# A new prologue order, a second issuer for a small load, and a split last copy in a fused attention and expert kernel on one core

## The chip, the cores and the metric

The kernel runs on one core of one Trainium2 chip. The core has five engines that matter here: TensorE (PE in the profile, with its weight loads as PEld), VectorE (DVE), ScalarE (ACT), GpSimd (POOL) and SyncE (SP). SP computes nothing in this kernel: it issues nearly all the transfers between the chip's main memory and the on-chip memory. Each engine takes its own instructions in the order in which the program lists them, and waits on semaphores for the others' results. The metric is the device time of one execution in microseconds; lower is better.

## The reference

There are 8 batches of 8 heads. Per head, `x` has 512 rows of 64 values and `state` 32 rows of 64. Rows of `x` attend to `state`, and rows of `state` attend to `x`; both results go, with the heads side by side, as 4352 rows of 512 values through a maxout layer:

```
scores = scale * x @ state.T              # 512 x 32 per head
a = softmax(scores);  xread = a @ state
scores2 = scale * state @ x.T             # the same products, transposed
a2 = softmax(scores2); sread = a2 @ x     # 32 x 64 per head
h = concat(xread, sread) over rows, heads side by side
out = maximum(h @ w1, h @ w2) @ w_out     # 512 -> 1024 -> 512
```

Inputs and output are float32.

## The kernel before

**The algebra.** The kernel never builds `h` for the `x` rows. Since `max(a, b) = relu(a - b) + b`, it forms `wd = w1 - w2` (tile `wd`, by `w_sub`) and `wwo = w2 @ w_out` (tile `wwo`, by `w_wo_mm` and `w_wo_ev`), so that `out = relu(h @ wd) @ w_out + h @ wwo`. And since `h = a @ state`, it multiplies the state of each batch into both matrices first (`sw_mm`, tile `sw`), after which a batch needs only its attention weights `a`, transposed (`aT`). Layer 1 is then `l1_mm` (line 426: two matmuls of 512 columns per 128 features) with a relu copy `l1_ev`; layer 2 is `l2_f` (line 442) plus `l2_open` (line 438) for the `wwo` part, both into one accumulator bank, copied out by `l2_out` and stored.

**The weights.** `w1`, `w2` and `w_out` come in four quarters (`load_w2(q)`, `load_w1(q)`, `load_wo(q)`, 512 KB each, lines 98 to 108). Quarter 0 comes in six half pieces of 256 KB (`load_h(j, w)`, lines 110 to 122; `w` is 2 for `w2`, 1 for `w1`, 0 for `w_out`). Each piece lands as float32 and is cast to bf16 by one of three engines: `w2_cast`, `wo_cast`, and for the halves `w2_cast_h`, `w1_cast_h`, `wo_cast_h`. The last letter of such a call is the engine: "A" ScalarE, "V" VectorE, "P" GpSimd. All these copies go through the helper `copy`, so that in the profile they stand under line 58 (ScalarE), 60 (VectorE) and 62 (GpSimd). For quarter 0 the difference is not needed: `sw_h_mm` (line 401) adds the products with `w1` and with the negated state and `w2`.

**The prologue** runs from the first instruction to `store(0)` and covers batch 0, the weights, and batch 1's attention. Its order is written out by hand, one call after another (lines 616 to 846); each call appends its instructions to the queues of its engines, so the list sets the order on every engine. Batch 0's `x` arrives in four pieces of two heads, and each goes through a cast (`cast_pair`), four transposes on PE (`xt_pair_mm`, line 200), a copy (`xt_pair_ev`), scores against the block-diagonal state (`scores_pair_mm`, line 218) and the exponential (`scores_pair_ev`). Weights go, quarter by quarter, through rounds: `w2_tr_mm(q)` transposes `w2`, `w_wo_mm(q, i)` (line 551) adds that quarter to `w2 @ w_out` for each of four row blocks `i` and needs the cast `wo(q)`; `sw_two_mm(q)` (line 387) needs `wd(q)`, the result of `w_sub(q)` (line 539), and makes the columns of `sw` for batches 0 and 1 together; two `l1_mm(0, f)` follow, and `l2_part(q, c)` (two matmuls of 512 columns, 573 to 576) adds the quarter to the four output accumulators `c` of batch 0. For quarter 0, `w_wo_h_mm(i, j)` (line 556) and `w2_tr_h_mm` (line 519) work by halves.

`idle(n)` (line 571) issues `n` matmuls of 256 columns on zeros. Their results are not used.

**The banks.** PE's results go to eight banks of accumulator memory, four in the pool `ps` and four in `pa`. A new result in a pool waits until an older one has been copied out. The four accumulators of `l2_part` take the `pa` banks.

**State.** Batches 0 and 1 have their own small loads (`load_state(0)`, `load_state(1)`, 64 KB each, line 127, issued by ScalarE), a cast (`copy(.., sb0[:, b], sf0[:, b])`), a transpose (`state_mm`, line 132) and two copies into the block-diagonal tile `sbd` (`state_ev`). `state0_neg` makes the negated copy for batch 0 (line 143). Batches 2 to 7 come together (`load_states`, `states_cast`, `states_mm`, `states_ev`).

**The transfers.** SP issues the loads in the order in which they are listed (579 to 606). A transfer's completion is signalled on one of eight semaphores taken in turn, so that each issue waits for the transfer eight places before it; some also wait until the buffer that they fill has been read. `load_w2(3)` fills the buffer that `w_sub(0)` reads last.

**The loop** over batches 1 to 7 (line 849) is the same for each: scores of the next batch, its softmax (`norm_sums`, `norm_mul`), its transposes by transfer, four layer 2 accumulators (`l2`), the next batch's `sw`, then its layer 1. In the last batch the rows of `sread` go through the layers as well (`moe_sread`), and the last accumulator is done in two halves of 256 columns, each copied out and stored by itself (`l2_last`, 456 to 469).

Of the kernel before, what the change touches and what calls it, by code (L numbers as in the profile page):

```python
# [15 lines left out]
def kernel(  # L16
# [107 lines left out]
    P = {}  # L124

    def load_state(b):
        nc.scalar.dma_start(out=sf0[:, b].rearrange("p (j d) -> p j d", j=2),
                            in_=state[b].rearrange("(k j) n d -> n k j d", j=2))
# [327 lines left out]
    def l2_last(b, c):  # L456

        dst = out[b * L:b * L + S].rearrange("(p c) n -> p c n", c=NC)
        for h in range(2):
# [8 lines left out]
            copy("AV"[h], OB[b][:, c, cs], p[:, 0:256])  # L468
# [111 lines left out]
    load_state(1)  # L580
# [3 lines left out]
    load_x(0, 4, 3)  # L584
    load_h(0, 2)
    load_h(0, 1)
    load_h(0, 0)
    load_h(1, 1)
    load_h(1, 2)
# [5 lines left out]
    load_w1(2)  # L595
    load_w2(3)
    load_wo(2)
# [18 lines left out]
    idle(15)  # L616
    cast_pair(0, 0, "V")
    copy("A", sb0[:, 0], sf0[:, 0])
    xt_pair_mm(0, 0, pa)
    cast_pair(0, 1, "V")  # L620
    idle(3)
    state_mm(0, None)
    xt_pair_ev(0, 0, "V")
    xt_pair_mm(0, 1, pa)
    copy("A", sb0[:, 1], sf0[:, 1])
    state_mm(1, pa)
    cast_pair(0, 2, "P")
    xt_pair_ev(0, 1, "V")
    state_ev(0, "A")
    idle(3)  # L630
    scores_pair_mm(0, 0, pa)
    cast_pair(0, 3, "V")
    xt_pair_mm(0, 2)
    xt_pair_ev(0, 2, "V")
    state_ev(1, "A")
    state0_neg("P")
    scores_pair_ev(0, 0)
    reduce_pair(0, 0)
    scores_pair_mm(0, 1, pa)
    scores_pair_ev(0, 1)  # L640
    reduce_pair(0, 1)
    w2_cast_h(0, "P")
    idle(1)
    xt_pair_mm(0, 3)
    norm_sums(0, 0, False)
    norm_mul(0, 0, "P")
    xt_pair_ev(0, 3, "A")
    idle(1)
    scores_pair_mm(0, 2, None)
    wo_cast_h(0, "P")  # L650
    scores_pair_ev(0, 2)
    reduce_pair(0, 2)
    idle(5)
    scores_pair_mm(0, 3, pa)
    scores_pair_ev(0, 3)
    w2_tr_h_mm(0)
    w1_cast_h(1, "P")
    w1_cast_h(0, "A")
    idle(3)
    sread_mm(0, pa)  # L660
    idle(3)
    sw_h_mm(0, pa)
    reduce_pair(0, 3)
    norm_sums(0, 1, False)
    norm_mul(0, 1, "V")
    w2_tr_h_ev(0, "A")
    sw_ev(0, 0, 128, 1, "A")
    idle(4)
    w_wo_h_mm(1, 0)
    at_mm(0, 0, pa)  # L670
    sw_ev(0, 0, 128, 0, "A")
    at_mm(0, 1)
    w_sub(0, 0, 4, "P")
    w_wo_h_mm(3, 0)
    w2_cast_h(1, "V")
    at_ev(0, 1, "V")
    sw_h_mm(1, pa)
    sw_ev(0, 128, 256, 1, "V")
    wo_cast_h(1, "V")
    w2_tr_h_mm(1)  # L680
    at_ev(0, 0, "A")
    l1_mm(0, 0)
    sw_ev(0, 128, 256, 0, "A")
    l1_mm(0, 1, pa)
    w_wo_h_mm(0, 0, pa)
    w2_tr_h_ev(1, "A")
    l1_ev(0, 1, "A")
    w_wo_h_mm(2, 0)
    l1_ev(0, 0, "V")
    w_wo_h_mm(3, 1)  # L690
    w_wo_ev(0, 3, "A")
    w2_cast(1, "P")
    w_wo_h_mm(0, 1)
    w_wo_h_mm(1, 1)
    w_wo_h_mm(2, 1)
    sread_norm(0)
    l2_part(0, 3)
    sw_mm(1, 0, FQ)
    w_wo_ev(0, 1, "A")
    sw_ev(1, 0, FQ, 1, "A")  # L700
    l2_part(0, 1)
    sw_ev(1, 0, FQ, 0, "A")
    l2_part(0, 0)
    w2_tr_mm(1)
    w_sub(1, 0, 4, "V")
    w2_tr_ev(1, "V")
    wo_cast(1, "P")
    sw_two_mm(1)
    sw_two_ev(1, 1, "V")
    w_wo_ev(0, 0, "A")  # L710
    l2_part(0, 2)
    w_wo_mm(1, 1)
    w_wo_ev(1, 1, "V")
    w_wo_ev(0, 2, "A")
    w_wo_mm(1, 2)
    sw_two_ev(1, 0, "A")
    l1_mm(0, 3)
    w2_cast(2, "P")
    l1_ev(0, 3, "A")
    l1_mm(0, 2)  # L720
    w_wo_mm(1, 3)
    w2_tr_mm(2)
    l1_ev(0, 2, "A")
    w_wo_ev(1, 2, "V")
    w_wo_mm(1, 0)
    l2_part(1, 1)
    w_sub(2, 0, 4, "V")
    l2_part(1, 0)
    w_wo_ev(1, 0, "V")
    w2_tr_ev(2, "A")  # L730
    sw_two_mm(2)
    sw_two_ev(2, 1, "A")
    sw_two_ev(2, 0, "A")
    l2_part(1, 2)
    w_wo_ev(1, 3, "V")
    w2_cast(3, "P")
    l2_part(1, 3)
    w_sub(3, 0, 4, "P")
    w2_tr_mm(3)
    l1_mm(0, 5)  # L740
    wo_cast(2, "V")
    w_wo_mm(2, 0)
    w_wo_ev(2, 0, "V")
    w2_tr_ev(3, "A")
    w_wo_mm(2, 2)
    l1_mm(0, 4)
    l1_ev(0, 5, "A")
    w_wo_mm(2, 3)
    w_wo_mm(2, 1)
    l1_ev(0, 4, "A")  # L750
    l2_part(2, 3)
    alloc_x(1, "P", big.tile([128, NC, 4, 132], BF16, tag="r", name="xo"))
    cast_pair(1, 1, "P")
    cast_pair(1, 0, "P")
    w_wo_ev(2, 2, "V")
    l2_part(2, 0)
    w_wo_ev(2, 3, "V")
    wo_cast(3, "A")
    sw_two_mm(3)
    sw_two_ev(3, 0, "A")  # L760
    w_wo_mm(3, 2)
    w_wo_ev(2, 1, "V")
    l2_part(2, 1)
    w_wo_mm(3, 0)
    sw_two_ev(3, 1, "V")
    cast_pair(1, 3, "P")
    l1_mm(0, 6)
    cast_pair(1, 2, "A")
    xt_mm(1, 0)
    w_wo_ev(3, 2, "V")  # L770
    w_wo_ev(3, 0, "V")
    xt_ev(1, 0, "V")
    l1_mm(0, 7)
    xt_mm(1, 1)
    l1_ev(0, 6, "A")
    l1_ev(0, 7, "A")
    xt_ev(1, 1, "A")
    w_wo_mm(3, 1)
    scores_mm(1, 0)
    w_wo_ev(3, 1, "V")  # L780
    w_wo_mm(3, 3)
    l2_part(3, 0)
    scores_mm(1, 1)
    l2_part(2, 2)
    states_cast("P")
    scores_ev(1, 0)
    cast_half(2, 0, "P")
    scores_ev(1, 1)
    w_wo_ev(3, 3, "V")
    sw_mm(0, FF, WC)  # L790
    sw_ev(0, FF, WC, 1, "A")
    sw_ev(0, FF, WC, 0, "A")
    norm_sums(1, 0)
    norm_mul(1, 0, "P")
    l2_part(3, 2)
    l2_part(3, 1)
    l2_part(3, 3)
    sw_mm(1, FF, WC)
    norm_sums(1, 1)
    sw_ev(1, FF, WC, 0, "A")  # L800
    sread_mm(1)
    norm_mul(1, 1, "P")
    l2_open(0, 3, ACC[3], False, True)
    l2_open(0, 2, ACC[2], False, True)
    l2_out(0, 3, ACC[3], "A")
# [110 lines left out]
```

## Time and profile before

| | us |
|---|---|
| median of 5 runs | 148.36 |
| the five runs | 147.72, 152.19, 148.66, 148.36, 147.77 |
| the profiled execution's own time | 147.72 |
| its span, first to last instruction | 145.9 |
| PE busy | 139.5 (96%) |
| DVE busy | 85.4 (58%) |
| ACT busy | 69.3 (47%) |
| POOL busy | 59.0 (40%) |
| first scores of batch 2 on PE (end of the prologue's part on PE) | 42.1 |
| end of PE's last matmul | about 142.6 |

All durations below come from the one profiled execution. Its page gives the busy time of each engine, the span cut into 40 slices of 3.65 us (each digit is the busy share of a slice in tenths), the chain of work that ended last, and groups of instructions by line. The trace behind it also lists each queue in order of time: start, duration, engine, line, operation, output tile and input tiles, shapes, and in brackets how long the engine sat idle before and what ended that. Matmuls are pipelined: one of 512 columns is listed with 0.38 us, but the next starts 0.216 us later, and some matmul records are missing. `idle` matmuls count as busy PE time.

### The profile page before, as it was taken

The numbers are of one execution on the slowest core, as the hardware profiler recorded it, in microseconds if no ns is written. First come the engines' busy times: TensorE is split into PE (matmuls) and PEld (weight loads), VectorE is DVE, ScalarE is ACT, GpSimd is POOL, SyncE is SP. The second block draws the span as 40 slices with busy tenths as digits, with TensorE's granted clock in tenths as the row PEclk, the third lists the DMA queues.
The fourth block names the chain that finished last, engine by engine and source line by source line (L and its number), as shares of the span: only waits on it lengthen the run. The fifth ranks groups of instructions, "written<-read, shape, count | busy, mean of one in ns | idle before, by whom it ended". The sixth has DMA issues, their size and how long they took to land.

```text
span 145.9 us, 3217 instructions
## 1 busy us (share of the span) xinstructions
PE 139.5 (96%) x1295; PEld 71.1 (49%) x1314; DVE 85.4 (58%) x172; ACT 69.3 (47%) x135; POOL 59.0 (40%) x80
## 2 busy tenths in 40 slices
PE   6998999999999999999999999999999999999990
PEld 4664454464554445444544544454445344754460
DVE  3499795877874648464854675376557464621111
ACT  4486857686971456326450825271537145511010
POOL 2289435767938433924291447226500500000000
PEclk9999999999999999999999999999999999999999
DMA  4999999994559988595948785787306032402423
GB/s 128 311 327 357 356 363 362 361 349 156 99 102 340 209 296 265 102 290 214 240 87 278 261 184 109 251 295 140 72 27 260 7 72 110 180 4 72 144 104 111
DMA packets 36639, 29.18 MB, mean 200 GB/s; under 512 B 20240, under 2 KB 33808, under 8 KB 35728
## 3 DMA queue, kind: packets, MB, share of 16 engines
q1 hardware_dynamic: 36080, 28.84, 66.7%
q8 instruction: 10, 0.16, 0.4%
q10 hardware_dynamic: 544, 0.13, 0.4%
q14 instruction: 5, 0.04, 0.1%
HBM read 15.34 MB, written 8.91 MB: 166 GB/s over the span
## 4 chain that ended last, share of the span: by engine, by line
PE 91%; DMA 3%; DVE 2%; issue 1%; ACTq 0%; ACT 0%
PE acc L442 37%; PE ps L426 17%; PE acc L438 8%; PE ps L551 4%; DMA sf<-in_state_dram 3%; PE ps L361 3%; PE ps L481 2%; PE acc L491 2%; PE ps L271 2%; PE acc L328 2%; PE acc L571 2%; PE acc L466 1%; DVE wo L60 1%; PE acc L426 1%; PE acc L489 1%
## 5 line engine op out<-in xcount | busy, mean ns | idle before, releaser
L442 PE MATMUL acc<-wo,r 128*128 128x512 bf16 x246 | 59.3, 379 | 0.4
L442 PEld LDWEIGHTS <-r 128*128 128x128 bf16 x248 | 23.8, 98 | 28.9 <-issue 0.6
L58 ACT COPY ob<-acc 128x512 f32<-128x512 f32 (+1 forms) x16 | 9.2, 572 | 48.1 <-PE acc L442 27.9
L426 PE MATMUL ps<-aT,sw 128*128 128x512 bf16 x117 | 27.7, 379 | 0.0
L294 POOL TENSOR_TENSOR a<-e,er 128x512 bf16<-128x512 bf16 x15 | 15.5, 1050 | 27.5 <-ACT e L276 20.8
L417 DVE TENSOR_SCALAR r<-ps 128x512 bf16<-128x512 f32 x26 | 18.0, 691 | 14.1 <-PE ps L426 14.0
L415 ACT ACTIVATE r<-ps 128x512 bf16<-128x512 f32 x33 | 19.7, 600 | 6.5 <-PE ps L426 5.8
L60 DVE COPY ob<-acc 128x512 f32<-128x512 f32 (+1 forms) x17 | 11.1, 652 | 16.0 <-PE acc L442 14.6
L426 PEld LDWEIGHTS <-sw 128*128 128x128 bf16 x128 | 12.1, 98 | 13.7
L62 POOL CAST xb<-xf 128x1024 bf16<-128x1024 f32 x12 | 12.4, 1040 | 15.3 <-DMA xf<-in_x_dram 15.3
L62 POOL CAST xo<-xf 128x512 bf16<-128x512 f32 x28 | 16.1, 615 | 6.0 <-DMA xf<-in_x_dram 5.6
L60 DVE CAST sw<-ps 128x512 bf16<-128x512 f32 x15 | 9.8, 687 | 12.0 <-PE ps L361 11.6
L438 PE MATMUL acc<-sw,aT 128*128 128x512 bf16 x49 | 15.5, 381 | 0.3
L58 ACT CAST sw<-ps 128x512 bf16<-128x512 f32 (+1 forms) x21 | 11.0, 573 | 2.5 <-PE ps L387 1.3
L287 DVE TENSOR_REDUCE es<-e 128x16 f32<-128x512 bf16 x14 | 9.2, 656 | 1.6 <-ACT e L276 1.6
L571 PE MATMUL acc<-wz 128*128 128x256 bf16 x38 | 7.5, 343 | 1.2 <-DVE ones L609 1.2
L276 ACT ACTIVATE e<-ps 128x512 bf16<-128x512 f32 x14 | 7.7, 597 | 0.8 <-PE ps L271 0.2
L438 PEld LDWEIGHTS <-aT 128*128 128x128 bf16 x62 | 5.0, 98 | 4.4
L551 PE MATMUL ps<-wo,w2t 128*128 128x512 bf16 x23 | 6.5, 380 | 0.2
L562 DVE TENSOR_TENSOR w2acc<-ps,w2acc 128x512 f32<-128x512 f32 x8 | 5.2, 687 | 1.6 <-PE ps L551 1.5
L539 POOL TENSOR_TENSOR wd<-w1f,w2f 128x1024 bf16<-128x1024 f32 x2 | 4.9, 2446 | 1.7 <-DMA w1f<-in_moe_w_dram 1.7
L571 PEld LDWEIGHTS <-wz 128*128 128x128 bf16 x38 | 4.1, 121 | 2.3 <-DVE ones L609 1.2
(111 smaller groups left out, 146.4 us busy)
## 6 DMA issues: line engine op xcount, KB each, us to landing
xf<-in_x_dram SPq DMA_DIRECT2D x14, 512.0 KB, 5.6
out_dram<-ob SPq DMA_DIRECT2D x7, 1024.0 KB, 4.2
w2f<-in_moe_w_dram SPq DMA_DIRECT2D x3, 512.0 KB, 7.6
w1f<-in_moe_w_dram SPq DMA_DIRECT2D x3, 512.0 KB, 9.4
wof<-in_moe_w_out_dram SPq DMA_DIRECT2D x3, 512.0 KB, 8.5
xf<-in_x_dram SPq DMA_DIRECT2D x4, 256.0 KB, 4.0
out_dram<-ob SPq DMA_DIRECT2D x3, 256.0 KB, 2.0
w2f<-in_moe_w_dram SPq DMA_DIRECT2D x2, 256.0 KB, 5.3
```

The lines of the kernel that those rows point to most:

```text
L58: nc.scalar.copy(o, i)
L60: nc.vector.tensor_copy(o, i)
L62: nc.gpsimd.tensor_copy(o, i)
L287: nc.vector.tensor_reduce(d["es"][:, hh], ev, axis=mybir.AxisListType.X, op=ALU.add)
L294: (nc.gpsimd if eng == "P" else nc.vector).tensor_mul(av, ev, d["er"][:, hh].unsqueeze(3).to_broadcast([128, 2 * NC, 2, Ns]))
L415: nc.scalar.activation(out=o, in_=p, func=ACTF.Relu)
L417: nc.vector.tensor_scalar(o, p, scalar1=0.0, scalar2=None, op0=ALU.max)
L426: nc.tensor.matmul(p, SW[b][:, g, f * 128:(f + 1) * 128], AT[b][:, g].rearrange("p c t -> p (c t)"), start=(g == 0), stop=(g == 1))
L438: nc.tensor.matmul(p, AT[b][:, g, c, :], SW[b][:, g, FF:WC], start=(start and g == 0), stop=(stop and g == 1))
L442: nc.tensor.matmul(p, R[b][:, f, c * 128:(c + 1) * 128], wo[:, f, :], start=(start and j == 0), stop=(stop and j == len(fs) - 1))
L551: nc.tensor.matmul(p, w2t[:, f, i, :], wo[:, f, :], start=(f == fs[0]), stop=(f == fs[-1]))
L571: nc.tensor.matmul(idle_p[0][:, 0:cols], wz[:, 0:128], wz[:, 0:cols], start=True, stop=True)
```

## The change

It has three parts.

1. `load_state(1)` is issued by SP instead of ScalarE, as the ninth of SP's loads. The half pieces of quarter 0 are loaded in another order (`w_out` first), and `load_wo(2)` goes ahead of `load_w2(3)`.
2. The whole list of the prologue is in another order, and some steps are on other engines. Moved to ScalarE: the casts of `w2` half 0 (from GpSimd), `w1` half 1 (from GpSimd) and `w_out` half 1 (from VectorE), and the negated state (from GpSimd). Moved to GpSimd: the casts of `w2` half 1 and of `w_out` quarter 2 (both from VectorE), and of state 1 (from ScalarE). Moved to VectorE: the cast of batch 0's third piece and one `norm_mul` of batch 1 (both from GpSimd). No weight cast is left on VectorE. There are 45 `idle` matmuls instead of 38. `sread_tr_mm(0)` goes from the end of the prologue to before `l1_mm(0, 0)`, and `l2_part(0, 2)` from round 0 to after `sw_two_ev(2, 0)`.
3. In `l2_last`, the last 256 columns are copied by ScalarE and VectorE, 128 columns each, instead of by VectorE alone.

```diff
-    def load_state(b):
-        nc.scalar.dma_start(out=sf0[:, b].rearrange("p (j d) -> p j d", j=2),
+    def load_state(b, q=nc.scalar):
+        q.dma_start(out=sf0[:, b].rearrange("p (j d) -> p j d", j=2),
...
-            copy("AV"[h], OB[b][:, c, cs], p[:, 0:256])
+            for e, c0, n in (("A", 0, 256),) if h == 0 else (("A", 0, 128), ("V", 128, 128)):
+                copy(e, OB[b][:, c, 256 * h + c0:256 * h + c0 + n], p[:, c0:c0 + n])
...
     load_state(0)
-    load_state(1)
     load_x(0, 4, 0)
...
+    load_h(0, 0)
     load_h(0, 2)
     load_h(0, 1)
-    load_h(0, 0)
+    load_h(1, 2)
+    load_state(1, nc.sync)
     load_h(1, 1)
-    load_h(1, 2)
     load_h(1, 0)
...
+    load_wo(2)
     load_w2(3)
-    load_wo(2)
```

The list after the change, from the first matmul to the end of round 1 on PE:

```
idle(15)
copy("A", sb0[:, 0], sf0[:, 0]); state_mm(0, None)
cast_pair(0, 0, "V"); state_ev(0, "A"); xt_pair_mm(0, 0, pa)
cast_pair(0, 1, "V"); idle(2); xt_pair_mm(0, 1)
state0_neg("A"); xt_pair_ev(0, 1, "A"); xt_pair_ev(0, 0, "V")
scores_pair_mm(0, 0, None); scores_pair_ev(0, 0)
cast_pair(0, 2, "V"); idle(2); xt_pair_mm(0, 2); xt_pair_ev(0, 2, "A")
scores_pair_mm(0, 1, pa); cast_pair(0, 3, "V"); idle(2); xt_pair_mm(0, 3, pa)
idle(3); scores_pair_mm(0, 2, pa); scores_pair_ev(0, 1); scores_pair_ev(0, 2)
reduce_pair(0, 0); xt_pair_ev(0, 3, "V"); idle(1)
scores_pair_mm(0, 3, pa); scores_pair_ev(0, 3)
w2_cast_h(0, "A"); idle(13); w2_tr_h_mm(0); sread_mm(0, pa); w1_cast_h(0, "A")
reduce_pair(0, 1); norm_sums(0, 0, False); w2_tr_h_ev(0, "A"); reduce_pair(0, 2)
idle(2); sw_h_mm(0, None); sw_ev(0, 0, 128, 0, "A"); sw_ev(0, 0, 128, 1, "A")
wo_cast_h(0, "P"); reduce_pair(0, 3); norm_sums(0, 1, False)
idle(4); w_wo_h_mm(2, 0, pa); norm_mul(0, 1, "V"); norm_mul(0, 0, "P")
w2_cast_h(1, "P"); w1_cast_h(1, "A"); at_mm(0, 0); at_mm(0, 1, pa)
copy("P", sb0[:, 1], sf0[:, 1]); state_mm(1, None); sread_norm(0)
w2_tr_h_mm(1, pa); w_wo_h_mm(1, 0, pa); w_sub(0, 0, 4, "P"); at_ev(0, 0, "V")
idle(1); sw_h_mm(1, None); w_wo_h_mm(3, 0); at_ev(0, 1, "A"); w2_tr_h_ev(1, "V")
w2_cast(1, "P"); sread_tr_mm(0, pa); wo_cast(1, "P"); l1_mm(0, 0, pa)
sw_ev(0, 128, 256, 1, "V"); sw_ev(0, 128, 256, 0, "A"); l1_mm(0, 1)
wo_cast_h(1, "A"); sread_tr_ev(0, "V"); l1_ev(0, 0, "A"); w_wo_h_mm(0, 0, pa)
state_ev(1, "V"); w_wo_h_mm(2, 1); w_wo_ev(0, 2, "A"); w_wo_h_mm(3, 1); w_wo_h_mm(0, 1)
sw_mm(1, 0, FQ); w_wo_h_mm(1, 1); sw_ev(1, 0, FQ, 0, "A"); w2_cast(2, "P")
l1_ev(0, 1, "V"); l2_part(0, 0); w_sub(1, 0, 4, "V"); w2_tr_mm(1)
sw_ev(1, 0, FQ, 1, "A"); l2_part(0, 3); w_wo_ev(0, 0, "A"); w2_tr_ev(1, "V")
sw_two_mm(1); l2_part(0, 1); w_wo_ev(0, 3, "A"); sw_two_ev(1, 1, "V")
w_wo_mm(1, 3); w_wo_ev(1, 3, "V"); sw_two_ev(1, 0, "A"); w_wo_mm(1, 1)
```

Before the change, the stretch that ends at the same place is this:

```
sw_h_mm(1, pa); sw_ev(0, 128, 256, 1, "V"); wo_cast_h(1, "V"); w2_tr_h_mm(1)
at_ev(0, 0, "A"); l1_mm(0, 0); sw_ev(0, 128, 256, 0, "A"); l1_mm(0, 1, pa)
...
w_wo_h_mm(3, 1); w_wo_ev(0, 3, "A"); w2_cast(1, "P")
w_wo_h_mm(0, 1); w_wo_h_mm(1, 1); w_wo_h_mm(2, 1); sread_norm(0)
l2_part(0, 3); sw_mm(1, 0, FQ); w_wo_ev(0, 1, "A"); sw_ev(1, 0, FQ, 1, "A")
l2_part(0, 1); sw_ev(1, 0, FQ, 0, "A"); l2_part(0, 0); w2_tr_mm(1)
w_sub(1, 0, 4, "V"); w2_tr_ev(1, "V"); wo_cast(1, "P"); sw_two_mm(1)
sw_two_ev(1, 1, "V"); w_wo_ev(0, 0, "A"); l2_part(0, 2); w_wo_mm(1, 1)
```

Further on, the rest of rounds 1 to 3 and batch 1's steps follow in both versions, in another order, with `l2_part(0, 2)` between `sw_two_ev(2, 0)` and `w_wo_mm(2, 3)`, `wo_cast(2, "P")` ahead of `w2_cast(3, "P")`, and `norm_mul(1, 1, "V")` after `norm_sums(1, 1)`.

## The prediction

> **What bounds the kernel now.** I read the page's slices first, then the chain that ended last, then the queues of the engines over the first 20 us.
>
> ```profile
> PE 139.5 (96%) x1295; PEld 71.1 (49%) x1314; DVE 85.4 (58%) x172; ACT 69.3 (47%) x135; POOL 59.0 (40%) x80
> PE   6998999999999999999999999999999999999990
> DMA  4999999994559988595948785787306032402423
> ```
>
> TensorE (PE) is full in every slice but the first, second and last, and a full slice may hold `idle` matmuls. The DMA engines are full for nine slices, about 33 us. The chain, asked over 10 to 20 us (start, duration, what), shows where the second slice's hole is:
>
> ```profile
> 12.42 0.29 DVE sw L60
> 12.71 1.73 DVE wo L60
> 14.45 0.04 issue
> 14.49 0.38 PE ps L556
> ...
> 17.63 0.70 DVE w2t L60
> 18.34 0.05 issue
> 18.38 1.04 PE ps L551 x4
> ```
>
> There are two stalls. At 14.49 PE waits 0.55 us for a VectorE weight cast. At 18.38 it starts round 1 of `w_wo_mm` (L551), and behind that start the chain names VectorE's `w2t` copy. But POOL's queue shows a second condition ending in the same moment:
>
> ```profile
> 11.63 2.53 POOL L539 TENSOR_TENSOR wd<-w1f,w2f 128x1024 bf16<-128x1024 f32 x1
> 14.11 1.23 POOL L62 CAST w2b<-w2f 128x1024 bf16<-128x1024 f32 x1
> 17.29 1.04 POOL L62 CAST wo<-wof 128x1024 bf16<-128x1024 f32 x1 [1.95 <-DMA wof<-in_moe_w_out_dram]
> 18.89 1.04 POOL L62 CAST w2b<-w2f 128x1024 bf16<-128x1024 f32 x1 [0.56 <-DMA w2f<-in_moe_w_dram]
> ```
>
> POOL sat 1.95 us until `wo(1)` landed at 17.29, and cast it until 18.33. L551 reads that tile, so it cannot start before about 18.38 however fast everything else is. The stretches confirm that the landing is set by bandwidth, not by issue (last columns: granted clock, DMA share, GB/s):
>
> ```profile
> 8.00:9.00 1.00, 1.00 (x19) 0.78 (x17) 0.85 (x3) 0.87 (x2) 0.61 (x1) 1.00 1.13 334
> 14.00:15.00 1.00, 0.51 (x3) 0.27 (x3) 1.00 (x3) 0.24 (x2) 1.00 (x2) 1.00 1.00 364
> 17.00:18.00 1.00, 1.00 (x26) 0.67 (x25) 0.49 (x2) 0.88 (x2) 0.71 (x1) 1.00 1.09 346
> ```
>
> After 18.38 PE is dense. I add up what it does until batch 2's first scores at 42.10: 84 matmuls of 512 columns at 0.216 (18.14), six groups of eight transposes at 0.45 (2.70), four groups of `sw` matmuls at 0.34 (1.36), scores, sread and two small transposes (0.93): 23.13 us of 23.72, the rest being about 0.1 after each group of narrow tiles. The loop from 42.10 to 142.5 repeats in 13.85 us without a hole. So time can come only from before 18.38, or from the tail.
>
> **The change part by part.**
>
> *Front, up to round 1.* PE's real work is the same in both orders, and up to round 1 it differs in one thing: ahead of its first `w_wo_mm(1,.)`, the old order has four `l2_part(0,.)`, the new one three; `l2_part(0,2)` now comes after `sw_two_ev(2,0)`. That is 2 x 0.216 = 0.43 us of PE work moved behind the 18.38 gate. In return `sread_tr_mm(0)`, one transpose (0.06), moves in front of it. If the gate stays, PE is 0.37 us behind from there on, and nothing after it has a hole to take that up.
>
> Does the gate stay? Ahead of `wo(1)` in the queue stand the same bytes: states 0 and 1 (0.13 MB), batch 0's x, the six half pieces and `w2(1)`, `w1(1)`; only their order differs, and the DMA engines are at 1.0 or above from 2 us on. I take 17.29 again. Bounds: POOL could be late by one 512 KB transfer's spacing (17.29 to 18.89, so 1.6 us at most); an earlier landing pays only until PE's own readiness, which is 17.98 (below), so it gains 0.40 at most.
>
> Is PE ready? My hand chain, with durations from the rows: x's third and fourth pieces land as now or a little sooner (6.3, 7.2); scores of pair 3 end at 8.9 (ACT's last `e` 9.4); ACT casts `w2` half 0 (0.61) to 10.0; 13 idles (0.107 each) hold PE to 10.25; transposes, sread, `sw_h_mm(0)` at 11.1; `w_wo_h_mm(2,0)` 11.8; `at_mm` 12.0; ACT casts `w1` half 1 after its two `sw` copies, 11.98 to 12.6; `sw_h_mm(1)` 13.1; `l1(0,0)`, `l1(0,1)` 13.65 to 14.5; ACT casts `wo` half 1 by 14.35, where VectorE now ends it at 14.44 (1.81 us, against 0.53 for its cast of `w2b` of the same size). This is where the exchanged casts meet: ScalarE takes three half-weight casts, `xt_ev` of pairs 1 and 2 and the negated state (0.4), and gives one state cast to POOL; VectorE loses two weight casts. So the removed slow cast is paid back nearly whole by a busier ScalarE: the new order's round 0 ends about where the old one does. `l2_part(0,3)` ends at 17.2; `wd(1)` is ready at 15.90 + 1.23 = 17.13 (VectorE, waiting on the same landing as now); `sw_two_mm(1)` 0.35, `l2_part(0,1)` 0.43: 17.98. It is 0.4 before the gate. The seven additional idles (38 to 45, 0.75 us) lie in waits for weights; with that cover gone they would cost 0.75 less the 0.4.
>
> At one place the trace speaks of a conflict. VectorE's 1.81 us cast ran wholly inside POOL's 2.53 us subtraction, and POOL's cast of `w1b` took 1.08 beside VectorE's `norm_mul`, against 0.61 alone. The Trainium skill, page "SBUF — State Buffer", says that the pair of ports which VectorE and GpSimd share is an exclusive lock, and that a VectorE instruction with two SBUF inputs contends with a GpSimd one that reads SBUF. By that rule the new order makes a new conflict: `norm_mul(1,1)` goes to VectorE (estimated 35.0) while POOL goes on to cast batch 2. A whole block of 1.04 by the rule would put it 0.2 past PE's arrival; by the 0.47 that the row shows it stays hidden.
>
> The sum goes without it: `at_mm(1,0)` needs `norm_mul(1,1)` at 36.8; 35.0 plus 0.96 is 35.96, cover 0.8. Loss bound, from VectorE's slowed cast (1.81 less 0.53, 1.28): 0.5.
>
> *State 1 on SP.* One issue of 0.68 leaves ACT's queue and ACT's table load (now from 2.15) starts that much sooner, but its next work is the state 0 cast, held by a landing at 3.94: worth nothing. SP's queue grows by 0.68 ahead of `w1` half 1 and the ten weight loads behind it. SP's issues now run more than 2 us ahead of the engines (`wo(1)` issued 8.51, landed 17.29), so 0.68 is covered; uncovered it costs 0.68. State 1 itself lands near 10.6 instead of 5.92. POOL casts it just before `w_sub(0)`, PE's `state_mm(1)` stands at 12.4 with `w2_tr_h_mm(1)` and the rest behind it: cover about 1 us.
>
> *Other moves.* `wo(2)` goes ahead of `w2(3)`, which waits 2.2 us on SP for POOL's `wd`; spacing of the landings (18.89, 21.89, 23.1) puts `wo(2)` at 21.9, POOL's cast at 22.9, PE's `w_wo_mm(2,3)` at about 23.5: cover 0.6. `w2(3)` at 23.1, cast by 24.2, read at 25.2. POOL's `w_sub(3)` ends at 27.0 in both; `sw_two_mm(3)` comes at 27.8. `states_cast`, batch 1's casts and the round 3 copies each keep 0.3 or more.
>
> *Tail.* The last 256 columns, 0.42 on VectorE (L60), become two 128-column copies side by side: VectorE 0.29 (its 128x128 `sw` row), ScalarE 0.27. Gain 0.13; bounds 0.15, and nothing if the store's wait for two engines takes it back.
>
> Sum: +0.43 - 0.06 - 0.13 = +0.24 us. The profiled execution took 147.72 (span 145.9), the fastest of the five, so 147.96 in its terms. The four runs without the 152.19 average 148.13, 0.41 above it, so I forecast 148.4 for a median.
>
> **The rivals.**
>
> *A late front (slower).* ScalarE takes over three half-weight casts (0.61 each) and works in order, so one late landing delays evictions behind it. If PE reaches `w_wo_mm(1,3)` after 18.9 instead of 17.98, more than the 0.4 of cover and 0.5 beyond, it decides. For it: ACT is 0.75 to 0.95 busy from 6 to 11 us already, and 13 idles in one block run whether needed or not. Against: the new order removes 1.28 of slowed cast. With 1.0 beyond the cover: 147.96 + 1.0, about 149.4 as a median.
>
> *A gate that opens early (faster).* `wo(1)` lands well before 17.29 because in truth the transfers are not served in order, and the front is 1 us ahead through the missing VectorE casts. Against: the DMA share above, and 14.35 against 14.44. Both would have to move to 17.3 for a gain of 0.8: 147.2, as a median 147.6.
>
> *No effect.* The moved `l2_part` falls into a hole that I don't see, or the gate varies by more than the term: 147.6 to 147.8, 148.1 as a median.
>
> **How the numbers follow.** Forecast 0.42, no effect 0.15, late front 0.31, early gate 0.12. A measurement here tells about 0.5% (0.74 us) from no change. The forecast and no effect end within it, save 0.03 at the slow edge; so same 0.54, slower 0.34, faster 0.12. The range: low lies just under the early gate's 147.6, at 147.5; high is the late front's 149.4 and some of the runs' spread (148.66 is 0.3 above the median), 149.6.
>
> **What would show it.** Right: POOL's `wo` cast still begins near 17.3 after a DMA wait, L551 (now L552) starts near 18.4 after PE has idled in all some 0.4 just before; batch 2's first scores near 42.5; the last VectorE copy near 0.29. Wrong: PE arrives at L552 with POOL's cast long done (late front), the cast starts before 16.5 (early gate), or a hole of 0.3 or more stands after 20 us, at `at_mm(1,0)` or `w_wo_mm(2,3)`.

## The result and the profile after

The changed kernel takes 148.69 us in the median (43 runs), the kernel before 148.28 us over 80 runs beside them. The ratio is 1.0028, with a 95% interval of 1.0017 to 1.0038: the change costs about 0.41 us (0.25 to 0.56). One run of the changed kernel took 820.28 us and seven of the 80 took 151 to 153; the ratios here leave such slow runs out, and those of the experiments are not the quotients of the two medians beside them. The profiled execution of the changed kernel took 149.00 us (span 147.2), a little above its median; that of before, 147.72, was near its fastest. So the two profiles differ by 1.28 us, three times what the change costs, and most of this section is about separating the two.

From the page after: the busy time of each engine, then PE's busy share and the DMA share in 40 slices.

```profile
PE 140.3 (95%) x1302; PEld 71.8 (49%) x1321; DVE 84.4 (57%) x174; ACT 70.0 (48%) x136; POOL 57.0 (39%) x78
PE   6988999999999999999999999999999999999990
DMA  4999999995459969496949594877307032402432
```

VectorE and GpSimd lost work (85.4 to 84.4 and 59.0 to 57.0), ScalarE gained 0.7, and none of this is on the path. PE's third slice (7.4 to 11.0 us) has lost a tenth, the fourth has its gap as before.

The chain of waits of the changed kernel between 12 and 20 us (start, duration, what):

```profile
12.69 0.24 PE acc L317 x4
12.93 0.02 issue
12.95 0.59 ACT aT L58
13.55 0.04 issue
13.59 0.38 PE acc L557
...
18.62 0.54 PE acc L442 x2
19.16 0.00 issue
19.16 1.02 PE ps L552 x4
```

The two stalls of before, VectorE's weight cast at 14.49 and its `w2t` copy ahead of round 1, are gone. In their place stands one wait, at 13.59: PE's `w_wo_h_mm(1, 0)` waits for ScalarE to copy out `at_mm(0, 1)`. Round 1 (L552) starts at 19.16, where before it started at 18.38.

GpSimd's queue in the changed kernel:

```profile
14.29 1.03 POOL L62 CAST w2b<-w2f 128x1024 bf16<-128x1024 f32 x1
18.07 1.04 POOL L62 CAST wo<-wof 128x1024 bf16<-128x1024 f32 x1 [2.75 <-DMA wof<-in_moe_w_out_dram]
19.69 1.04 POOL L62 CAST w2b<-w2f 128x1024 bf16<-128x1024 f32 x1 [0.57 <-DMA w2f<-in_moe_w_dram]
```

Here `wo(1)` landed at 18.07, not at 17.29, and its cast ended at 19.11. PE came to the same place at about 18.99 (its last pair of `l2_part` matmuls is listed from 18.55, and such a pair takes 0.44 until the next group, as the same pair does in the run with the old load list below, 18.75 to 19.19). Both conditions of round 1 are late in this execution: the cast by 0.8 against the 18.33 of before, PE by 1.0 against the 17.98 of the prediction.

The end of the kernel, last accumulator: the last copy before the change, then what stands there after it, copy by copy:

```profile
142.59 0.42 DVE L60 COPY ob<-acc 128x256 f32<-128x256 f32 x1 [1.49 <-PE acc L466]
```

```profile
142.75 0.93 PE L466 MATMUL acc<-wo,r 128*128 128x256 bf16 x7
...
143.72 0.27 ACT L58 COPY ob<-acc 128x128 f32<-128x128 f32 x1 [0.72 <-PE acc L466]
144.02 0.29 DVE L60 COPY ob<-acc 128x128 f32<-128x128 f32 x1 [1.79 <-ACT ob L58]
```

The two copies of 128 columns do not run side by side. VectorE's waits for ScalarE's, so together they take 0.59 us (143.72 to 144.31); the one copy of 256 columns before took 0.42. All six profiles with the new tail have this order, with the same 0.27 and 0.29.

**What separates the change from the run.** Three instants carry it: the cast of batch 0's last piece of `x` on VectorE (`xo`), the start of round 1 on PE (L551, L552 after the change), and the first scores of batch 2 on PE (L271; their first row before is at 41.97, the 42.1 of the table ahead of the prediction). Of all kernels run here, with the profiled execution's own time:

| kernel | `x` cast | round 1 | difference | scores | difference | time | time less scores |
|---|---|---|---|---|---|---|---|
| before | 7.18 | 18.38 | 11.20 | 41.97 | 23.59 | 147.72 | 105.75 |
| changed | 7.45 | 19.16 | 11.71 | 43.09 | 23.93 | 149.00 | 105.91 |
| b_defer | 8.16 | 19.47 | 11.31 | 43.49 | 24.02 | 149.24 | 105.75 |
| b_defer2 | 6.94 | 18.32 | 11.38 | 42.34 | 24.02 | 148.12 | 105.78 |
| a_fill | 6.91 | 18.92 | 12.01 | 42.42 | 23.50 | 148.32 | 105.90 |
| a_loads | 7.65 | 19.19 | 11.54 | 43.12 | 23.93 | 149.03 | 105.91 |
| a_tail | 7.17 | 18.71 | 11.54 | 42.65 | 23.94 | 148.41 | 105.76 |
| a_state | 7.88 | 20.77 | 12.89 | 44.70 | 23.93 | 150.62 | 105.92 |
| a_bank | 6.72 | 18.53 | 11.81 | 42.47 | 23.94 | 148.38 | 105.91 |
| a_idle | 7.01 | 18.45 | 11.44 | 42.38 | 23.93 | 148.29 | 105.91 |
| best | 6.81 | 18.58 | 11.77 | 42.08 | 23.50 | 147.82 | 105.74 |
| best2 | 7.32 | 18.73 | 11.41 | 42.24 | 23.51 | 148.03 | 105.79 |
| best3 | 6.20 | 17.86 | 11.66 | 41.61 | 23.75 | 147.36 | 105.75 |

The last column has only two values: 105.74 to 105.79 where VectorE copies the last 256 columns alone, 105.90 to 105.92 where two engines share them. So the new tail costs 0.15 us, in every execution, and everything else that varies lies before the scores of batch 2. The sixth column is 23.50 to 23.59 where `l2_part(0, 2)` stands ahead of round 1 and 23.93 to 24.02 where it stands behind; best3, with the step ahead, has 23.75, 0.2 of it in a gap of PE at 30.1 us that best2 does not have. What is left, and what differs from run to run, is when `x` lands and how long PE takes from there to round 1.

With these two constants a measured ratio can be split. The change costs 0.41; 0.16 of it is the tail (105.91 less 105.75), 0.34 lies between round 1 and the scores (23.93 less 23.59), and so -0.09 is left for the start of round 1. In the median, round 1 starts as early as before. I use the same split, 148.28 times the ratio less 1, for the experiments; it assumes that the two constants of a kernel's profile hold for its other runs.

### The profile page after: what moved, and what is told of

Its sections match the earlier page's. It is cut to its first block, busy times and chain, and to the rows that moved or that the text cites. A ratio compares the mean times of both kernels' runs of the same rounds, so it can differ in the third digit from the quotient of the medians.

```text
span 147.2 us, 3235 instructions
## 1 busy us (share of the span) xinstructions
PE 140.3 (95%) x1302; PEld 71.8 (49%) x1321; DVE 84.4 (57%) x174; ACT 70.0 (48%) x136; POOL 57.0 (39%) x78
## 4 chain that ended last, share of the span: by engine, by line
PE 91%; DMA 4%; issue 1%; SPq 1%; ACT 1%; DVE 0%
PE acc L442 37%; PE ps L426 18%; PE acc L438 9%; PE ps L552 4%; DMA xf<-in_x_dram 4%; PE ps L361 3%; PE ps L482 2%; PE acc L492 2%; PE ps L271 2%; PE acc L572 2%; PE acc L328 2%; PE acc L466 1%; PE acc L490 1%; PE acc L557 1%; SPq L91 1%
## 5 line engine op out<-in xcount | busy, mean ns | idle before, releaser
L58 ACT COPY ob<-acc 128x512 f32<-128x512 f32 (+2 forms) x18 | 9.9, 556 | 49.5 <-PE acc L442 27.8
L417 DVE TENSOR_SCALAR r<-ps 128x512 bf16<-128x512 f32 x29 | 20.0, 691 | 14.6 <-PE ps L426 14.4
L294 POOL TENSOR_TENSOR a<-e,er 128x512 bf16<-128x512 bf16 x14 | 14.4, 1049 | 29.3 <-ACT e L276 20.4
L415 ACT ACTIVATE r<-ps 128x512 bf16<-128x512 f32 x32 | 19.0, 600 | 6.4 <-PE ps L426 4.6
L60 DVE COPY ob<-acc 128x512 f32<-128x512 f32 (+1 forms) x16 | 10.3, 643 | 16.7 <-PE acc L442 14.6
L60 DVE CAST sw<-ps 128x512 bf16<-128x512 f32 (+1 forms) x16 | 10.1, 663 | 12.3 <-PE ps L361 11.0
L58 ACT CAST sw<-ps 128x512 bf16<-128x512 f32 (+2 forms) x24 | 11.7, 535 | 3.6 <-PE ps L387 2.0
L572 PE MATMUL acc<-wz 128*128 128x256 bf16 x45 | 8.4, 329 | 1.2 <-DVE ones L610 1.2
L62 POOL CAST wo<-wof 128x1024 bf16<-128x1024 f32 (+1 forms) x3 | 2.7, 896 | 11.2 <-DMA wof<-in_moe_w_out_dram 11.2
L552 PE MATMUL ps<-wo,w2t 128*128 128x512 bf16 x23 | 6.4, 379 | 0.1
L572 PEld LDWEIGHTS <-wz 128*128 128x128 bf16 x45 | 4.8, 118 | 2.8 <-DVE ones L610 1.2
```

Source lines behind the costliest of these rows:

```text
L58: nc.scalar.copy(o, i)
L60: nc.vector.tensor_copy(o, i)
L62: nc.gpsimd.tensor_copy(o, i)
L294: (nc.gpsimd if eng == "P" else nc.vector).tensor_mul(av, ev, d["er"][:, hh].unsqueeze(3).to_broadcast([128, 2 * NC, 2, Ns]))
L415: nc.scalar.activation(out=o, in_=p, func=ACTF.Relu)
L417: nc.vector.tensor_scalar(o, p, scalar1=0.0, scalar2=None, op0=ALU.max)
```

## The experiments

After the first trace two readings of the front stood against each other. *Late loads*: the new order of the loads, with state 1 on SP, brings `wo(1)` late (18.07 against 17.29). *Late front*: PE itself comes late, through the wait at 13.59, wherever `wo(1)` is. Besides, each of the three parts was to be priced by itself.

**1. b_defer: the moved step alone, in the kernel before.**

```diff
     sw_two_ev(1, 1, "V"); w_wo_ev(0, 0, "A")
-    l2_part(0, 2)
     w_wo_mm(1, 1)
...
     sw_two_ev(2, 0, "A")
+    l2_part(0, 2)
```

> The kernel before with one edit: the two matmuls of l2_part(0,2) go behind sw_two_ev(2,0), as in the changed kernel. Moved-work theory: they leave a place ahead of the gate (POOL's cast of wo(1)) where PE waits anyway, and come back where PE is dense, so the kernel is 0.43 us slower, ratio about 1.003, and first scores of batch 2 come 0.43 later with the wo(1) cast where it was. Late-loads theory (the changed kernel is slower because its load list lands wo(1) later): no part of the slowdown here, ratio 1.000. Late-front theory (PE itself is late at the gate): removing 0.43 ahead of the gate starts round 1 earlier by as much, ratio 1.000.

Measured: 148.90 against 148.06, ratio 1.0062 (1.0041 to 1.0083). Twice what the step weighs, and more than any of the three readings expected. After round 1 the trace has just the step: 24.02 less 23.59 is 0.43. The rest came ahead of it. VectorE's and GpSimd's casts of the last two pieces of `x`, in b_defer:

```profile
7.46 0.61 POOL L62 CAST xo<-xf 128x512 bf16<-128x512 f32 x1 [6.01 <-DMA xf<-in_x_dram]
8.16 0.55 DVE L60 CAST xo<-xf 128x512 bf16<-128x512 f32 x1 [2.19 <-DMA xf<-in_x_dram]
```

Both wait for their landing, and the last comes 0.98 us later than before's 7.18, though no load was touched. So single profiles, and even a handful of runs, hold a variation of the landings as large as what is sought.

**2. a_fill: the changed kernel with that step moved back ahead of round 1.** `w_wo_ev(0, 1)`, which the step reads, goes ahead as well, and `w2_tr_mm(2)` takes a bank of the other pool.

```diff
-    sw_two_ev(2, 0, "A"); l2_part(0, 2)
+    sw_two_ev(2, 0, "A")
...
     w_wo_ev(0, 3, "A")
+    w_wo_ev(0, 1, "A")
     sw_two_ev(1, 1, "V")
+    l2_part(0, 2)
     w_wo_mm(1, 3); w_wo_mm(1, 1)
-    w_wo_ev(0, 1, "A")
...
-    w2_tr_mm(2, pa)
+    w2_tr_mm(2)
```

> The changed kernel with l2_part(0,2) back ahead of the first w_wo_mm of round 1 (its bank freed by taking w_wo_ev(0,1) one place up on ScalarE; w2_tr_mm(2) takes a ps bank). Moved-work theory: 0.37 to 0.43 us faster than the changed kernel, ratio to before about 0.999 to 1.000. Late-front theory: PE has no hole there, so nothing changes, ratio stays at 1.003. Late-loads theory: nothing changes beyond 0.1, ratio 1.003.

Measured: 148.68 against 148.06, ratio 1.0058 (1.0038 to 1.0078). No gain. PE in a_fill, up to round 1:

```profile
17.70 0.41 PE L387 MATMUL ps<-wd,sbd 64*32 64x256 bf16 x16
18.05 1.04 PE L442 MATMUL acc<-wo,r 128*128 128x512 bf16 x4
18.92 0.81 PE L552 MATMUL ps<-wo,w2t 128*128 128x512 bf16 x3
```

The four matmuls stand directly against round 1. `wo(1)` landed at 17.36 and was cast by 18.40, so there was no hole for the step to fall into: PE was late by itself. The interval after round 1 shrank to 23.50, as it should, and the front grew to 12.01, which is 11.58 and the step's 0.43. What the step gave behind the gate it took in front of it. The ratio is worse than that: it lies 0.0030, some 0.4 us, above the changed kernel's, which no reading expected and the trace, at 148.32 the fastest of its six runs, does not show. That is as much as b_defer had too much, on the same chip beside it.

**3. a_loads: the changed kernel with the whole old list of loads.**

```diff
     load_state(0)
+    load_state(1)
     load_x(0, 4, 0)
...
-    load_h(0, 0)
     load_h(0, 2)
     load_h(0, 1)
-    load_h(1, 2)
-    load_state(1, nc.sync)
+    load_h(0, 0)
     load_h(1, 1)
+    load_h(1, 2)
     load_h(1, 0)
...
-    load_wo(2)
     load_w2(3)
+    load_wo(2)
```

> The changed kernel with the whole load list of before: state 1 issued by ScalarE, w2 half first, w2(3) ahead of wo(2). Late-loads theory: wo(1) lands near 17.3 again instead of 18.07, batch 2's first scores come 0.8 us sooner, ratio about 0.998. Moved-work theory: the landing of wo(1) varies from run to run and the list has no part in it; ratio stays within 0.001 of 1.003, unless a half piece that now comes later (w_out half 0) holds PE in the first 14 us.

Measured: 148.86 against 148.06, ratio 1.0068 (1.0047 to 1.0089), slower than the changed kernel, whose interval ends at 1.0038. *Late loads*, which expected a gain, falls. `wo(1)` landed at 17.24 here and was cast by 18.50, yet PE came to round 1 at 19.19, 11.54 us after the last piece of `x`. The same 11.54 stands in a_tail, with the new loads, and in the changed kernel (18.99 less 7.45). This is the front's own length, with either list of loads. Over all profiles the cast of `wo(1)` starts at 17.31 on average with state 1 on ScalarE's queue (five) and at 17.48 with it on SP's (eight). By the split, round 1 came 0.5 later than in the kernel before (148.28 x 0.0068 is 1.01, less 0.50). But a_fill, run beside it with the new loads, is at 1.0058, so this ratio alone does not price the loads.

**4. a_tail: the changed kernel with the last 256 columns on VectorE alone.**

```diff
-            for e, c0, n in (("A", 0, 256),) if h == 0 else (("A", 0, 128), ("V", 128, 128)):
-                copy(e, OB[b][:, c, 256 * h + c0:256 * h + c0 + n], p[:, c0:c0 + n])
+            copy("AV"[h], OB[b][:, c, cs], p[:, 0:256])
```

> The changed kernel with the last 256 columns copied by VectorE alone, as before. In the changed kernel's profile VectorE's 128 columns wait for ScalarE's: 0.27 + 0.30 in series against 0.42. If that is the rule and not the one profile: the stretch from the last matmul to the last copy's end shrinks by 0.15 to 0.17 us and the ratio to before falls by 0.001, to about 1.002. If the two copies usually run side by side: 0.13 us slower than the changed kernel, ratio 1.004.

Measured: 148.41 against 148.06, ratio 1.0026 (1.0005 to 1.0048). The ratio cannot tell 0.15 us from the changed kernel's 1.0028. The trace can: VectorE's last copy in a_tail is one instruction of 0.42, which waits for PE,

```profile
143.28 0.42 DVE L60 COPY ob<-acc 128x256 f32<-128x256 f32 x1 [1.49 <-PE acc L466]
```

and the time less the scores fell from 105.91 to 105.76. The table's last column shows the same in all thirteen executions.

**5. a_state: the changed kernel with state 1 alone back on ScalarE's queue.**

```diff
     load_state(0)
+    load_state(1)
     load_x(0, 4, 0)
...
-    load_state(1, nc.sync)
```

> The changed kernel with state 1's load alone put back on ScalarE's queue, second there; all else of the new list stays. Front theory (x's last piece sets the pace of the first 18 us, and state 1 ahead of it delays it): the third and fourth pieces are cast 0.3 to 0.6 us later than 6.2 and 7.2, round 1 starts as much later, ratio to before 1.005 to 1.007. Rival (the order of the half pieces, and not state 1, made the kernel with the old load list slower): pieces land as in the changed kernel, ratio 1.003.

Measured: 149.18 against 148.44, ratio 1.0067 (1.0036 to 1.0097). About 0.6 us above the changed kernel, as a_loads was, though the lower end of its interval touches the changed kernel's; the split gives the same 0.5 for round 1. a_bank and a_idle below, run beside it on the same chip with state 1 on SP, took 148.45 and 148.46. In its trace `x` came late (7.16 and 7.88), and what followed on PE was out of the ordinary:

```profile
7.65 0.40 PE L200 MATMUL ps<-ident,xo 128*128 128x128 bf16 x4 [1.67 <-DVE xo L60]
...
10.15 2.18 PE L572 MATMUL acc<-wz 128*128 128x256 bf16 x13
```

Thirteen `idle` matmuls took 2.18 us, where they took 1.58 in the changed kernel. The profiled run was the slowest of its eight (150.62; the others 148.76 to 149.26), so this is not what the median shows. The landing of `x` can be compared over the profiles: over the five with state 1 on ScalarE's queue the last `x` cast starts at 7.56 on average (6.94 to 8.16), over the eight with state 1 later, on SP's, at 6.95 (6.20 to 7.45). The ranges overlap. One thing does not: SP's four issues of `x`, from 0.73, take 2.16 to 2.18 us in the five profiles and 1.99 to 2.00 in the eight, so that the last piece is issued about 0.17 later with state 1 on ScalarE's queue. The rest of the 0.6 is not shown to be state 1's.

**6. a_bank: the changed kernel with `w_wo_h_mm(1, 0)` two steps later.** It takes the bank that `at_mm(0, 1)` filled.

```diff
     w2_tr_h_mm(1, pa)
-    w_wo_h_mm(1, 0, pa)
     w_sub(0, 0, 4, "P"); at_ev(0, 0, "V")
     idle(1); sw_h_mm(1, None); w_wo_h_mm(3, 0)
+    w_wo_h_mm(1, 0, pa)
     at_ev(0, 1, "A")
```

> The changed kernel with w_wo_h_mm(1,0) moved behind w_wo_h_mm(3,0) on PE, so that sw_h_mm(1) no longer stands behind its wait for the bank of at_mm(0,1). Front theory: sw_h_mm(1) starts 0.4 to 0.8 us earlier after x's last piece; round 1 starts earlier by 0.1 to 0.4, until POOL's cast of wo(1) is the next wait; ratio 1.000 to 1.002. Rival (the gate at wo(1), as forecast): the front has cover, ratio stays at 1.003.

Measured: 148.45 against 148.44, ratio 1.0019 (0.9997 to 1.0041), not to be told from the changed kernel's. But the trace shows what it did. `sw_h_mm(1)` starts at 12.51, 5.79 after the last `x` cast, against 6.55 in the changed kernel: 0.76 won. PE in a_bank then runs into the two weight waits:

```profile
16.40 0.59 PE L442 MATMUL acc<-wo,r 128*128 128x512 bf16 x2
17.40 0.41 PE L387 MATMUL ps<-wd,sbd 64*32 64x256 bf16 x16 [0.40 <-DVE wd L540]
17.74 0.60 PE L442 MATMUL acc<-wo,r 128*128 128x512 bf16 x2
18.53 1.02 PE L552 MATMUL ps<-wo,w2t 128*128 128x512 bf16 x4 [0.19 <-POOL wo L62]
```

This is much the picture that I had forecast for the changed kernel: `wd(1)` late, then the cast of `wo(1)`, landed at 17.44, and round 1 at 18.53. The gate is real, and stands right behind the front's own hold. Taking that away alone gives little.

**7. best: the bank, the fill and the old tail together**, the edits of experiments 2, 4 and 6 in one kernel.

> The changed kernel with three edits: w_wo_h_mm(1,0) behind w_wo_h_mm(3,0), l2_part(0,2) ahead of round 1's first w_wo_mm (w_wo_ev(0,1) one place up, w2_tr_mm(2) in a ps bank), and the last 256 columns copied by VectorE alone. Front theory: 0.17 at the end, and 0.3 to 0.4 because the two matmuls now fill the wait for wo(1): about 0.6 to 0.8 us faster than the changed kernel, ratio 0.997 to 0.999. If the bank's wait only moves on to another bank: ratio 1.002, as with the tail alone.

Measured: 148.07 against 148.44, ratio 0.9990 (0.9970 to 1.0010). That is 0.38 below a_bank, whose edit it includes and which ran beside it on the same chip. In the two traces the tail gives 0.17 (105.91 to 105.74) and the step 0.39, since it now falls into the hole that experiment 6 opened (23.94 to 23.50 behind round 1, with round 1 at 18.58 against 18.53). The step's cover exists once the front's hold is gone.

**8. a_idle: the changed kernel with fewer `idle` matmuls.**

```diff
-    idle(13)
+    idle(8)
...
-    idle(2); sw_h_mm(0, None)
+    sw_h_mm(0, None)
...
-    idle(4); w_wo_h_mm(2, 0, pa)
+    idle(2); w_wo_h_mm(2, 0, pa)
```

> The changed kernel with nine idle matmuls less between the last scores and w_wo_h_mm(2,0) (13 to 8, 2 to 0, 4 to 2). If the idles hold up the front: w2_tr_h_mm(0) starts right after ScalarE's cast of w2 half 0 and round 1 up to 0.3 us earlier, ratio 1.000 to 1.002. If they only fill waits for the weights, or PE's clock falls without them: no gain, ratio 1.003 or more.

Measured: 148.46 against 148.44, ratio 1.0028 (1.0006 to 1.0049): no gain over the changed kernel. In PE's queue the wait at the bank doubled (ScalarE copied `at_mm(0, 1)` out behind its cast of `w1` half 1, which had waited 0.43 for its landing),

```profile
12.78 0.38 PE L557 MATMUL acc<-wo,w2t 128*128 128x512 bf16 x1 [0.83 <-ACT aT L58]
```

and round 1 then started at 18.45, 0.05 after the end of the cast of `wo(1)` (17.36 and 1.04). So the `idle` matmuls taken out had stood in time that PE would have waited anyway, at the bank or at the gate.

**9. best2: best, with two `l2_part` ahead of `sw_two_mm(1)`, and the cast of `wo(1)` halved between GpSimd and ScalarE.**

```diff
-    wo_cast(1, "P")
+    copy("P", wo[:, 2, :], wof[1][:, 0, :])
...
     w_wo_ev(0, 0, "A")
+    w_wo_ev(0, 1, "A")
+    l2_part(0, 1)
+    l2_part(0, 2)
     w2_tr_ev(1, "V"); sw_two_mm(1)
-    l2_part(0, 1)
     w_wo_ev(0, 3, "A")
-    w_wo_ev(0, 1, "A")
+    copy("A", wo[:, 3, :], wof[1][:, 1, :])
     sw_two_ev(1, 1, "V")
-    l2_part(0, 2)
```

> The kernel of run best with two more edits: l2_part(0,1) and l2_part(0,2) stand ahead of sw_two_mm(1) on PE (w_wo_ev(0,1) right behind w_wo_ev(0,0) on ScalarE), and the cast of wo(1) is halved between GpSimd and ScalarE. If the gate theory is right, PE's wait for wd(1) of about 0.3 is filled and the gate opens 0.4 earlier, at the landing plus 0.61 instead of plus 1.04: round 1 starts near 18.1 to 18.2 instead of 18.58, 0.4 us faster than best, ratio to before 0.995 to 0.997. If another wait (a bank, VectorE's w2t copy) stands behind it, round 1 starts at 18.4 to 18.6 as in best, ratio 0.999.

Measured: 147.92 against 148.17, ratio 0.9986 (0.9963 to 1.0009), not separable from best, and short of the 0.995 to 0.997 expected. PE ran from 15.66 to round 1 at 18.73 without a hole, so in this execution the front, behind an `x` that came at 7.32, was the limit again; the halves of `wo(1)` were ready at 18.65, just ahead of it.

**10. b_defer2: experiment 1 once more**, the same edit, to learn whether its excess belonged to the edit.

> The same edit as run b_defer (the kernel before with l2_part(0,2) behind sw_two_ev(2,0)), whose time came out 0.9 us above the kernel before while its trace after round 1's start shows 0.43 more. If the rest was x's pieces landing late by chance: x's last piece is cast near 7.2 again and the ratio falls to 1.003. If it is a part of the edit: the front is late again and the ratio stays at 1.006.

Measured: 148.41 against 148.17, ratio 1.0028 (1.0005 to 1.0050), which is 0.42 us, the step's 0.43. Behind round 1 the trace again has 24.02. The last `x` cast started at 6.94 this time, and round 1 at 18.32:

```profile
17.47 0.41 PE L387 MATMUL ps<-wd,sbd 64*32 64x256 bf16 x16
18.32 1.04 PE L551 MATMUL ps<-wo,w2t 128*128 128x512 bf16 x3 [0.44 <-DVE w2t L60]
```

So the excess of experiment 1 did not belong to the edit; its one profile puts it down to the late `x`. A second thing is to be seen here: `wo(1)` landed at 17.00 and was cast by 18.04, and still PE waited until 18.32, for VectorE's `w2t`. That copy waits for PE itself, for its transposes of `w2` (L532):

```profile
17.57 0.69 DVE L60 COPY w2t<-ps 128x1024 bf16<-128x1024 bf16 x1 [0.88 <-PE ps L532]
```

In b_defer it is the same: the cast of `wo(1)` ended at 18.99, and round 1 started at 19.47, behind `w2t`. Counted from the end of the last `x` cast, round 1 comes 10.77 later in the kernel before, 10.76 in b_defer and 10.76 in b_defer2, wherever the cast of `wo(1)` ends. So in the old order it was the front, through `w2t`, that set round 1; in the profile of before the cast of `wo(1)` only ended at the same time. By the same count the front of the changed kernel, of a_loads and of a_tail takes 11.11.

**11. best3: best2 with the fewer `idle` matmuls of experiment 8.**

> The kernel of run best2 with the nine idle matmuls of run a_idle taken out as well. In best2 PE goes without a hole from 15.7 to round 1 at 18.73, 11.4 after its last x piece was cast, while wo(1)'s halves were ready at 18.65. If the idles are what still holds the front: round 1 starts 10.9 to 11.1 after the last x piece, 0.2 to 0.4 us earlier than in best2 for the same landing, and the ratio to before is 0.995 to 0.997. If the front then only waits longer for the landing of w1 half 1 and for wd(1), as when the idles alone were taken out: ratio 0.998 to 0.999, as best and best2.

Measured: 147.56 against 148.14, ratio 0.9969 (0.9948 to 0.9989). It is faster than the kernel before by 0.46 us (0.16 to 0.77) and so than the changed kernel too; its interval overlaps best2's, so what the `idle` matmuls alone gave is open. Its round 1, on PE and then on GpSimd:

```profile
17.16 0.41 PE L387 MATMUL ps<-wd,sbd 64*32 64x256 bf16 x16
17.86 0.81 PE L551 MATMUL ps<-wo,w2t 128*128 128x512 bf16 x3 [0.29 <-POOL wo L62]
```

```profile
17.20 0.61 POOL L62 CAST wo<-wof 128x512 bf16<-128x512 f32 x1 [2.68 <-DMA wof<-in_moe_w_out_dram]
```

With the bank's hold, the `idle` matmuls and half of the cast gone, PE stands at round 1 waiting for the landing at 17.20 and 0.61 of cast. Round 1 comes 11.66 after the `x` cast, not the 10.9 to 11.1 expected, because it is the gate that holds it here. `x` came at 6.20 in this execution, the earliest of all, so that PE's early arrival is in part luck.

## Why the prediction was right or wrong

The forecast of 148.4 lies 0.3 us below the measured 148.69, inside the range, and the sign of the sum was right. Half of the 0.3 is the base: the four runs averaged 148.13, the 80 have 148.28 in the median. By its terms, as the split gives them, it looks less good:

| term | predicted | measured |
|---|---|---|
| `l2_part(0, 2)` behind the gate, `sread_tr_mm(0)` in front | +0.37 | +0.34 |
| start of round 1 | 0 | -0.09 |
| tail | -0.13 | +0.16 |
| sum | +0.24 | +0.41 |

**Right: the moved step.** 0.34 in the changed kernel, 0.43 alone in the kernel before (b_defer2), and 0.43 back in a_fill's and best's stretch behind round 1. PE is dense there, and the step costs its full work. No hole came in the loop, and the time less the scores shows that to 0.05 us. What the step had filled in the old order was PE's wait for `w2t`, though, as b_defer and b_defer2 show, and not one for `wo(1)`.

**Right: the smaller covers.** `norm_mul(1, 1)` did come under GpSimd's casts of batch 2: VectorE needed 0.88 from 35.96, GpSimd's two casts 2.49 instead of 2.08, which is 0.41 lost in the 0.61 that they ran beside it. `at_mm(1, 0)` started at 37.47 without a wait, as the reckoning from the trace's row had it, and not 0.2 late. `wo(2)`, `w2(3)` and the casts of the states left no wait either.

**Wrong, the tail.** The step was "two 128-column copies side by side". They are in series, ScalarE 0.27 and then VectorE 0.29, since VectorE's copy waits for ScalarE's. I had bounded this from below at nothing ("if the store's wait for two engines takes it back") and had not let it be a loss. The two copies share their accumulator bank and their output tile; which of the two makes the wait was not tried. The same profile speaks for the bank: two copies out of two banks into halves of one tile `sw` do overlap,

```profile
14.38 0.27 ACT L58 CAST sw<-ps 128x128 bf16<-128x128 f32 x1 [0.84 <-PE ps L401]
14.42 0.29 DVE L60 CAST sw<-ps 128x128 bf16<-128x128 f32 x1 [0.76 <-PE ps L401]
```

so a shared output tile alone does not put them in series. This term was off by 0.29 us, more than any other line of the table.

**Wrong, and cancelled: the start of round 1.** It was costed at nothing through two steps, and that it came out near nothing is luck. The first, "Is PE ready?", put PE at 17.98, which is 10.78 behind an `x` cast at 7.2. The changed kernel, a_loads and a_tail all take 11.54, so PE needs 0.76 us more than I said, and the cover of 0.4 ahead of the gate does not exist. Nor does the new round 0 end "about where the old one does": from the end of the `x` cast the new front is 0.35 longer (11.11 against 10.76). The place is known: `sw_h_mm(1)` stood at 13.1 in my chain and came at 14.00, 0.65 later when counted from `x`, behind `w_wo_h_mm(1, 0)`. I had listed that matmul's weights and not its bank, which `at_mm(0, 1)` had just filled and which ScalarE had to copy out (0.59) first. a_bank won 0.76 there and had PE waiting for the gate again. This is the mechanism of the *late front* rival in a small size, though not by late evictions of the weights. The second step, state 1 on SP, "worth nothing", was probably a gain. With state 1 back on ScalarE's queue (a_loads, a_state) round 1 comes 0.5 later than in the kernel before; with it on SP, in the same front, 0.09 earlier (the changed kernel) and 0.03 later (a_tail). That is about 0.5 us, and the last `x` piece is 0.6 earlier on average in the traces. Against it stands a_fill, with state 1 on SP: by the split its round 1 is 0.8 later, of which the step explains 0.43. I had looked for what else ScalarE's queue would start sooner, found nothing, and not asked whom the 64 KB delayed on the way. The traces show 0.17 of it, in SP's issues of `x`. That the rest is the transfer's sharing of the DMA engines is argued and not shown, and that state 1 is its cause is likely and not shown.

**The gate: right for the new order, wrong for the old.** a_bank, a_idle and best3 start round 1 within 0.05 us of the end of the cast of `wo(1)`. But that L551 was held by it in the kernel before is a reading of one profile in which two waits end together; in b_defer and b_defer2 the front, through `w2t`, ends 0.48 and 0.28 later. In the new order PE's own arrival is beside the gate, and all three lie within some 0.5 us, less than the landings vary. *Early gate* would have needed PE at 17.3, and the landing too; the earliest landing seen was 17.00. *No effect* is excluded by the interval, although the prediction had held that less than 0.74 us could not be told from no change.

Of the signs named, only the last one came as written in the profile after, VectorE's copy of 0.29: the cast of `wo(1)` began at 18.07 (17.3 was named), L552 at 19.16 (18.4) after a wait of less than 0.2, and the scores at 43.09 (42.5).

Four readings in the prediction are off, and none of them carries the sum. PE's hole is in the fourth slice (10.9 to 14.6 us), not the second. The DMA engines are full for eight slices, 29 us, not nine. VectorE's cast of 1.81 ran from 12.63 to 14.44, so its end lies 0.28 behind the end of GpSimd's subtraction at 14.16, not wholly inside it. And the scores of batch 2 start at 41.97, not 42.10, so that the dense stretch is 23.59 long.

What stays open: the front's loss of 0.5 (a_loads, a_state) and state 1's gain of 0.5 are each known to 0.2 or 0.3 at best, since they are differences of ratios whose intervals are about 0.3 wide on each side, and b_defer and b_defer2, one kernel, differ by 0.5. That is as much as either of the two.

## What to carry to other kernels

Before a moved or added PE step is costed, write down its bank beside its inputs: which result lies there, which engine copies it out, and when. Two copies of one accumulator given to two engines are worth a split only if the trace of any such pair shows them overlapping; here the pair ran in series. Before a wait is named the gate, look whether another ends in the same moment, and take a second profile: here the two came apart in the next one. When a profile varies, look for two instants after which the time is constant, as the time less the scores of batch 2 was here: that tells a term of 0.15 us which no ratio could, and shows which part of the span the variation sits in.

## What the runs showed of the hardware

**A small early load is not free for its neighbours.** With one 64 KB load (256 rows of 256 bytes) in the second place of ScalarE's queue, SP's four issues of `x` took 2.16 to 2.18 us in five profiles; with it in the ninth place of SP's they took 1.99 to 2.00 in eight. The time differed by about 0.5 us of 148 in two pairs of runs (a_loads and a_state against the changed kernel), but a_fill does not fit, and the share of the load in it is not shown.

**Most of the spread goes with the landings of the first 8 us.** b_defer and b_defer2, the same kernel, had their last `x` cast at 8.16 and 6.94 us and took 149.24 and 148.12 us. The last `x` cast started between 6.20 and 8.16 us in 13 executions, and from the scores of batch 2 on all of them agree to 0.05 us within a tail's kind.

**The clock dropped once after a wait.** In a_state PE waited 1.67 us for the third piece of `x`, and the granted clock fell. Stretches of 3 and 4 us of a_state (each engine's busy time, then the granted clock, the DMA share and GB/s):

```profile
5.00:8.00 3.00, 1.32 (x20) 0.81 (x19) 0.96 (x4) 1.53 (x4) 0.00 (x0) 1.00 1.04 331
8.00:12.00 4.00, 4.00 (x35) 3.08 (x33) 3.20 (x9) 2.67 (x6) 2.30 (x4) 0.58 1.15 321
12.00:16.00 4.00, 3.60 (x94) 2.43 (x91) 2.04 (x7) 2.12 (x5) 3.96 (x3) 1.00 1.01 350
```

It was 0.58 from 8 to 12 us, where the changed kernel had 1.00, and it cost that execution more than 1 us (round 1 at 12.89 after `x`, not 11.54). In the changed kernel PE's waits in the same stretch were 0.33 and 0.47 us, and the clock held. One execution shows the order of the two, not that the wait was the cause. b_defer speaks against the wait alone: there PE waited 1.57 us, until 7.08, and was busy for 1.14 us of the stretch from 5 to 8 us, against 1.32 in a_state, and the granted clock stayed at 1.00 up to 12 us.
